# One core, two decode attention blocks: the V product as a loop of four passes, and projections over two banks

## The chip, the core and the metric

The kernel runs on one core of a Trainium2 chip. Five engines work beside each other and meet only at semaphores: TensorE (PE in the profile; its weight loads are listed apart as PEld), VectorE (DVE), ScalarE (ACT), GpSimd (POOL) and SyncE (SP). Here SyncE issues every transfer. The time of a run is what the device takes for one execution, in microseconds (us).

## What is computed

Two independent blocks, A and B, do the same with their own weights and caches. Each takes one new token for two batch entries, projects it to 32 query heads, attends over 8192 cached positions for each head and batch entry, and projects the result back; the two outputs stand side by side.

```python
q = (x @ wq).reshape(B, Sq, H, Dh).transpose(0, 2, 1, 3)     # B=2, Sq=1, D=640, H=32, Dh=192
scores = jnp.einsum("bhqd,bhkd->bhqk", q, k_cache) * (Dh ** -0.5)   # 8192 keys
p = softmax(scores, axis=-1)
o = jnp.einsum("bhqk,bhkd->bhqd", p, v_cache)
out = o.transpose(0, 2, 1, 3).reshape(B, Sq, H * Dh) @ wo
```

Every head has its own keys and values, and there is one query for each, so the caches are read once: 64 units of two heads and one batch entry, each with 6144 KB of K and 6144 KB of V, in bfloat16.

## The kernel before

**Units.** A unit u is two heads of one batch entry; u runs from 0 to 63, block A first. The 128 partitions hold 64 for each of the two heads; each partition holds 128 positions of 192 values.

**Buffers and loads.** Three buffers of 6144 KB each take the loads in the order k0, k1, v0, k2, v1, k3, v2 and so on. The list is written out, and load i waits until load i-3 has been used up (`done(i - NBUF)`): for K that is the unit's last product on VectorE (`dve_mul`, line 288), for V its product on TensorE (`pe_pv`, line 379). The first K load goes out at once. The loads k1 and v0 wait for the 16th and the 32nd projection instead, since their buffers hold the projection weights until then. The output weights `wo` come last, into buffers as these come free. All of them are issued by SyncE from line 247.

**Projections** (before the units). For each of 32 pairs of heads `pe_q` (line 357) makes five matmuls into one PSUM bank. VectorE copies two quarters of the bank to `qall` (`dve_qx`, line 278), and then ScalarE the other two (`act_q`, line 283). The banks are taken in turn from the list `qps`, which has four: the three score banks and `outps`. The projection hp waits for ScalarE's copy of hp-4, by the key `("qa", hp - NQ)` with `NQ = len(qps)`. On each engine this runs as a hardware loop, four pairs of heads in a turn, and the address of `wq` is taken from a register.

**One unit.** VectorE multiplies K by q in four chunks (line 288; two product buffers). TensorE sums each chunk with 12 matmuls against the identity (`pe_sum`, line 365), and VectorE reduces the result to scores (line 292). Then come the maximum (line 298), the maximum over partitions on GpSimd (line 269), and the exponential on ScalarE with sums over rows in `rs` (line 327). TensorE makes the denominator with `pe_l` (line 371), and the weighted sum of V with `pe_pv`: 64 matmuls, with 34 columns of `pb` as weights and 384 columns of V moving. VectorE and ScalarE put the result together (lines 303, 306, 309, 312).

**The order on TensorE** is fixed by a table of slots: in slot u the four chunk sums of unit u, then `pe_l` and `pe_pv` of unit u-1. Slots run in a hardware loop of three units a turn, since the buffers come round in threes; inside it all addresses of the chunk sums and of `pe_pv` are constants. A wait inside a loop is against a register, worked out from the turn's number (`_emit`, line 110; the loop itself is line 65).

**The end.** After the last K the products with V of units 62 and 63 remain, then `pe_turn` (line 393), which transposes the heads' results, and the output projections `pe_out` (line 407), block A and then block B. Between the two, `pe_idle` (line 415) makes eight matmuls whose result nobody reads.

Of the kernel before, what the change touches and what calls it, by code (L numbers as in the profile page):

```python
# [9 lines left out]
F32 = mybir.dt.float32  # L10


class _Stream:
# [93 lines left out]
    def _emit(self, eng, ops, it=None, steps=None):  # L107
        for fn, need, inc, _ in ops:
            for sid, (sem, val) in need.items():
                eng.wait_ge(sem, val if it is None else it * steps[sid] + val)  # L110
            if fn is None:
                continue
            ins = fn(eng)
            if inc:
                ins.then_inc(self.sem, inc)


def build_kernel(nc, blocks, out):
# [6 lines left out]
    NCH = T // TC  # L125
    TJ = T // 2
# [7 lines left out]
    NU = NP * B  # L134
    LASTU = NU - 1
    scale = float(Dh) ** -0.5
    NBUF = 3
    MP = 34
    JB = 16
    QW = 2 * Dh  # L140
# [6 lines left out]
    with ExitStack() as es:  # L147
        sb = lambda name, shape, dt: es.enter_context(nc.sbuf_tensor(name, shape, dt))
# [5 lines left out]
        ones = sb("ones", [128, 1], F32)  # L154
        big = sb("big", [128, NBUF * BUFE + 2 * PRODE], BF16)
        qall = sb("qall", [128, NU, Dh], BF16)
        pb = [sb(f"pb{i}", [128, 2 * T], BF16) for i in range(3)]
# [3 lines left out]
        mp = [sb(f"mp{i}", [128, 2], F32) for i in range(3)]  # L161
        mg = [sb(f"mg{i}", [128, 2], F32) for i in range(3)]
        nb = [sb(f"nb{i}", [128, 1], F32) for i in range(3)]
        rs = [sb(f"rs{i}", [128, 2], F32) for i in range(3)]
        ident = sb("ident", [128, 128], BF16)
        tri = sb("tri", [HP, HP + 1], BF16)
        place = sb("place", [2, 256], BF16)
# [4 lines left out]
        ops = [ps(f"ops{i}", [128, 512], F32) for i in range(3)]  # L172
        scps = [ps(f"scps{i}", [128, TC, DG], F32) for i in range(3)]
        outps = ps("outps", [128, 512], F32)
        oTps = ps("oTps", [128, 512], F32)
        qbank = [t[:].rearrange("p a b -> p (a b)") for t in scps]
        oacc = [outps[:], qbank[(LASTU * NCH + 1) % 3]]
        qps = qbank + [outps[:]]
        NQ = len(qps)

        kv = [big[:, i * BUFE:(i + 1) * BUFE].rearrange("p (t d) -> p t d", d=Dh) for i in range(NBUF)]
# [33 lines left out]
        buf = {}  # L215
# [8 lines left out]
        woA, wo0, wo1 = bk * BUFE, b62 * BUFE, b63 * BUFE  # L224
# [13 lines left out]
        def key(name, *idx):  # L238
            return (name,) + tuple(idx)

        def back(name, u, c, n):
            i = u * NCH + c - n
            return (name, i // NCH, i % NCH) if i >= 0 else None
# [24 lines left out]
        def pool_ar(u):  # L268
            return lambda eng: eng.partition_all_reduce(mg[u % 3][:], mp[u % 3][:], 128, bass.bass_isa.ReduceOp.max)  # L269
# [16 lines left out]
        def dve_mul(u, c):  # L286
            t = kv[buf["k", u]]
            return lambda eng: eng.tensor_tensor(prod[c % 2], t[:, c * TC:(c + 1) * TC, :],  # L288
                                                 qall[:, S_dve.at(u), :].broadcast_to([128, TC, Dh]), ALU.mult)

        def dve_red(u, c):
            return lambda eng: eng.tensor_reduce(sc[u % 3][:, c * TC:(c + 1) * TC], scps[(u * NCH + c) % 3][:], AXL.X, ALU.add)  # L292

        def dve_max(u):
            def fn(eng):
                for s in range(2):
                    r = slice(64 * s, 64 * s + 64)
                    ins = eng.tensor_reduce(mp[u % 3][r, s:s + 1], sc[u % 3][r, :], AXL.X, ALU.max)  # L298
                return ins
            return fn  # L300

        def dve_rc(u):
            return lambda eng: eng.reciprocal(rc[u % 3][:], ops[u % 3][0:2, QW:QW + 1])  # L303

        def dve_ohi(u):
            return lambda eng: eng.tensor_copy(o_hi[:], ops[u % 3][32:34, Dh:QW])  # L306
# [7 lines left out]
        def act_nb(u):  # L314
            def fn(eng):
                for s in range(2):
                    r = slice(64 * s, 64 * s + 64)
                    ins = eng.activation(nb[u % 3][r, :], mg[u % 3][r, s:s + 1], ACTF.Identity, scale=-scale)  # L318
                return ins
            return fn  # L320
# [41 lines left out]
        def pe_sum(u, c):  # L362
            def fn(eng):
                for j in range(NJ):
                    ins = eng.matmul(scps[(u * NCH + c) % 3][:], ident[:], prod[c % 2][:, :, j * DG:(j + 1) * DG],  # L365
                                     start=(j == 0), stop=(j == NJ - 1))
                return ins
            return fn

        def pe_l(u):  # L370
            return lambda eng: eng.matmul(ops[u % 3][0:2, QW:QW + 1], rs[u % 3][:], ones[:], start=True, stop=True)  # L371

        def pe_pv(u):
            vv = kv[buf["v", u]].rearrange("p (j a) d -> p j (a d)", a=2)

            def fn(eng):
                for j in range(TJ):
                    j0s = 4 * JB * (j // JB) + 2 * (j % JB)
                    ins = eng.matmul(ops[u % 3][0:MP, 0:QW], pb[u % 3][:, j0s:j0s + MP], vv[:, j, :],  # L379
                                     start=(j == 0), stop=(j == TJ - 1))  # L380
                return ins
            return fn

        def pe_turn(heads, blks):
# [15 lines left out]
        def pe_out(n):  # L400
# [8 lines left out]
                                         start=(i == 0), stop=(i == WR - 1))  # L409
                return ins  # L410
            return fn

        def pe_idle(eng):
            for i in range(8):
                ins = eng.matmul(ops[(LASTU + 1) % 3][:], ident[:], big[:, woA + 512 * i:woA + 512 * (i + 1)], start=True, stop=True)
            return ins

        NSLOT = NU + 8
        tabs = {e: {} for e in ("dve", "act", "pe", "pool")}
# [1 line left out]
        def put(eng, slot, order, fn, waits, sig, tag=None):  # L421
            t = tabs[eng].setdefault(slot, [])
            t.append((order, len(t), fn, waits, sig, tag))
# [14 lines left out]
        for u in range(NU):  # L438
            for c in range(NCH):
                w = [("k", u), ("pq", NP - 1), ("qa", NP - 1), ("qx", NP - 1), back("s", u, c, 2)]  # L440
                slot, order = (0, 9.2) if (u, c) == (1, 0) else (u, 2 + 2 * c)
                put("dve", slot, order, dve_mul(u, c), w, ("m", u, c), ("m", c, u % 3))
                put("dve", u, 5 + 2 * c if c < NCH - 1 else 9.5, dve_red(u, c),
                    [("s", u, c), key("mx", u - 3), key("exp", u - 3)], ("r", u, c), ("r", c, u % 3))
                put("pe", u, 0.1 * c, pe_sum(u, c),
                    [("m", u, c), ("os", -2) if (u, c) == (1, 0) else None, back("r", u, c, 3), ("id1",), ("qx", NP - 1), ("qa", NP - 1)], ("s", u, c), ("s", c, u % 3))
            put("dve", u, 12, dve_max(u), [("r", u, NCH - 1), key("ar", u - 3), ("init",)], ("mx", u), ("mx", u % 3))
            put("pool", u, 0, pool_ar(u), [("mx", u), key("nb", u - 3)], ("ar", u), ("ar", u % 3))
            put("act", u, 0, act_nb(u), [("ar", u), key("exp", u - 3)], ("nb", u), ("nb", u % 3))
            put("act", u, 1, act_exp(u), [("nb", u), key("pv", u - 3), key("l", u - 3), ("init",)], ("exp", u), ("exp", u % 3))  # L450
            w0 = [("exp", u), key("os", u - 3), key("rc", u - 3), ("init",)]
            pslot = u + 1
            pe_o = 2
            put("pe", pslot, pe_o, pe_l(u), w0, ("l", u), ("l", u % 3))
            put("pe", pslot, pe_o + 0.1, pe_pv(u), [("v", u)], ("pv", u), ("pv", u % 3, buf["v", u]))
            put("dve", u + 2, 20, dve_rc(u), [("pv", u), key("of", u - 3)], ("rc", u), ("rc", u % 3))
            put("dve", u + 2, 21, dve_ohi(u), [("pv", u), key("os", u - 1)], ("oh", u), ("oh", u % 3))
            put("dve", u + 2, 22, dve_osum(u), [("oh", u), key("of", u - 1)], ("os", u), ("os", u % 3))
            put("act", u + 2, 4, act_of(u), [("os", u), ("rc", u)], ("of", u), ("of", u % 3))

        put("pe", 0, -1, None, [("init",)], None)
        E2 = NU + 2
# [10 lines left out]
        for n, p in enumerate(pieces):  # L473
# [1 line left out]
            if p[0]:  # L475
                w.append(("r", LASTU, 1))
            put("pe", E2, 0.01 * n if n <= NA else 2 + 0.01 * n, pe_out(n), w, ("f", n))
        put("pe", E2, 1, pe_idle, [("of", LASTU)], None)
        for blk, n in enumerate((NA, len(pieces) - 1)):
            put("act", E2, 9 + blk, out_half(blk, 0), [("f", n)], ("oev", blk, 0))  # L480
            put("dve", E2 + 2, 30 + blk, out_half(blk, 1), [("f", n)], ("oev", blk, 1))
# [32 lines left out]
        for n in range(128 // HP):  # L514
# [9 lines left out]
            "dve": lambda u: [("m", u, 0), ("m", u, 1), ("r", u, 0), ("m", u, 2), ("r", u, 1), ("m", u, 3),  # L524
                              ("r", u, 2), ("r", u, 3), ("mx", u), ("rc", u - 2), ("oh", u - 2), ("os", u - 2)],
            "act": lambda u: [("nb", u), ("exp", u), ("of", u - 2)],
            "pe": lambda u: [("s", u, c) for c in range(NCH)] + [("l", u - 1), ("pv", u - 1)],
            "pool": lambda u: [("ar", u)],
        }
        pre, post = {}, {}  # L530
        for name, keys in per_unit.items():
            pre[keys(0)[0]] = [k for u in (-3, -2, -1) for k in keys(u)]
            for u in range(3):
                late = [k for k in keys(u) if k[1] < 0]
                if late:
                    post[[k for k in keys(u) if k[1] >= 0][-1]] = late

        for name, S in (("dve", S_dve), ("act", S_act), ("pe", S_pe), ("pool", S_pool)):
            for slot in sorted(tabs[name]):
                for _, _, fn, waits, sig, tag in sorted(tabs[name][slot], key=lambda e: (e[0], e[1])):  # L540
                    S.add(fn, waits=waits, sig=sig, tag=(slot, tag if tag is not None else object()),
                          pre=pre.get(sig, ()), post=post.get(sig, ()))
# [73 lines left out]
```

## Time and profile before

| what | value |
|---|---|
| time, median of 3 runs | 1936.92 us (1936.66 to 1936.93) |
| span of the profiled execution, first to last instruction | 1935.4 us |
| bytes moved, mean rate | 836.91 MB, 432 GB/s |
| share of the span that the DMA queue's packets took | 99.9% |
| TensorE matmuls busy | 1501.1 us (78%) |
| VectorE busy | 1122.5 us (58%) |
| mean granted TensorE clock | 0.956 |

The device time of the profiled execution is not listed apart from its span. The runs are 1.3 to 1.5 us longer than that span; this is what lies around the first and last instruction.

A row of a timeline gives start, length (both us), engine, line, operation, output and inputs, the number of instructions, and in brackets the idle time before it and what ended that. A row for a line of the kernel gives the shortest, median and longest duration in ns and where in the span the first and the last instruction started. Names ending in q (PEldq, SPq) are an engine's sequencer: register operations, branches and the issue of transfers, which do not count as busy.

### The profile page before, as it was taken

What the parts mean: (1) busy time and instruction counts of PE and PEld (TensorE: products, weight loads), DVE (VectorE), ACT (ScalarE), POOL (GpSimd) and SP (SyncE); (2) the same over time, 40 slices, a digit from 0 to 9 for tenths busy, and PEclk for the clock granted to TensorE, in tenths of its full rate; (3) what the DMA queues carried; (4) which work ended last, traced back from release to release, by engine and by line L of the source; (5) the groups of instructions that cost most, each with busy time, mean ns of one, the idle gap of its engine ahead of it and who ended that gap; (6) DMA issues with size and microseconds to landing.
All of it is one profiled execution on the core that took longest, in us unless ns stands there. A gap on an engine that the chain in (4) does not pass through costs nothing.

```text
span 1935.4 us, 19060 instructions
## 1 busy us (share of the span) xinstructions
PE 1501.1 (78%) x7728; PEld 730.0 (38%) x7729; DVE 1122.5 (58%) x907; ACT 142.4 (7%) x519; POOL 28.5 (1%) x113
## 2 busy tenths in 40 slices
PE   5788878878878878877877877877877877877878
PEld 2334433433433433433433333433333433433434
DVE  4765565565565565565565565565565565565560
ACT  3100000000000000000000000000000000000000
POOL 0000000000000000000000000000000000000000
PEclk9899999999999999999999999999999999999998
DMA  9999999999999999999999999999999999999999
GB/s 423 424 435 437 431 434 437 432 433 437 436 429 436 437 430 435 436 432 433 437 435 431 436 435 430 436 437 430 435 437 430 434 438 435 430 436 436 429 436 394
DMA packets 19754, 836.91 MB, mean 432 GB/s; under 512 B 2200, under 2 KB 2336, under 8 KB 2720
## 3 DMA queue, kind: packets, MB, share of 16 engines
q1 hardware_dynamic: 19744, 836.78, 99.9%
q8 instruction: 6, 0.10, 0.0%
q14 instruction: 4, 0.03, 0.0%
HBM read 836.77 MB, written 0.01 MB: 432 GB/s over the span
## 4 chain that ended last, share of the span: by engine, by line
DMA 49%; PE 28%; DVE 17%; issue 5%; DVEq 0%; SPq 0%; ACT 0%; ACTq 0%
DMA big<-in_B_k_cache_dram 25%; DMA big<-in_A_k_cache_dram 22%; PE ops L379 18%; DVE big L288 15%; PE scps L365 8%; DVE sc L292 2%; DMA big<-in_B_wo_dram 1%; PE scps L357 1%; DMA xw<-in_B_x_dram 1%; PE outps L357 0%; PE ops L371 0%; DVEq L288 0%; DVE qall L278 0%; SPq L247 0%; PE scps L407 0%
## 5 line engine op out<-in xcount | busy, mean ns | idle before, releaser
L288 DVE TENSOR_TENSOR big<-big,qall 128x6144 bf16<-128x6144 bf16 x256 | 852.8, 3351 | 526.6 <-DMA big<-in_B_k_cache_dram 278.7
L365 PE MATMUL scps<-big,ident 128*128 128x512 bf16 x3072 | 771.8, 408 | 401.1 <-DVE big L288 398.7
L379 PE MATMUL ops<-big,pb 128*34 128x384 bf16 x4096 | 676.8, 326 | 0.0
L365 PEld LDWEIGHTS scps<-big,ident 128*128 128x128 bf16 x3072 | 301.1, 104 | 865.1 <-DVE big L288 491.0
L379 PEld LDWEIGHTS ops<-big,pb 128*34 128x34 bf16 x4096 | 395.5, 98 | 258.7
L292 DVE TENSOR_REDUCE sc<-scps 128x32 f32<-128x512 f32 x256 | 175.8, 687 | 192.5 <-PE scps L365 192.5
L318 ACT ACTIVATE nb<-mg 64x1 f32<-64x1 f32 x128 | 25.8, 201 | 1706.8 <-POOL mg L269 1706.1
L327 ACT ACTIVATE pb<-sc,nb 64x128 bf16<-64x128 f32 x128 | 55.8, 436 | 7.8
L269 POOL PARTITION_ALL_REDUCE mg<-mp x64 | 25.7, 402 | 1857.9 <-DVE mp L298 1857.9
L298 DVE TENSOR_REDUCE mp<-sc 64x1 f32<-64x128 f32 x128 | 35.9, 280 | 8.3
L312 ACT ACTIVATE qall<-o_sum,rc 2x192 f32 (+1 forms) x64 | 29.0, 453 | 20.7 <-DVE o_sum L309 19.1
L309 DVE TENSOR_TENSOR o_sum<-ops,o_hi 2x192 f32<-2x192 f32 x64 | 22.1, 345 | 7.7
L357 PE MATMUL scps<-big,xw 128*128 x120 | 23.2, 351 | 2.2 <-DVE xw L274 2.2
L327 ACT ACTIVATION_READ_ACCUMULATOR pb<-sc,nb 64x1 f32 x128 | 23.7, 185 | 0.0
L306 DVE COPY o_hi<-ops 2x192 f32<-2x192 f32 x64 | 22.3, 349 | 2.0
L303 DVE RECIPROCAL rc<-ops 2x1 f32<-2x1 f32 x64 | 10.0, 156 | 21.3 <-PE ops L379 19.4
L278 DVE CAST qall<-scps 64x192 f32 x48 | 17.0, 355 | 6.5 <-PE scps L357 4.5
L283 ACT ACTIVATE qall<-scps 64x192 f32 x48 | 15.6, 324 | 30.1 <-DVE qall L278 27.8
L348 PE MATMUL oTps<-ident,xw 4*128 4x4 bf16 x5 | 0.4, 178 | 21.7 <-DMA xw<-in_B_x_dram 21.7
L357 PEld LDWEIGHTS scps<-big,xw 128*128 128x128 bf16 x120 | 12.4, 103 | 11.4 <-issue 5.2
L371 PEld LDWEIGHTS ops<-ones,rs 128*2 128x2 f32 x128 | 5.5, 82 | 26.9 <-issue 26.9
L407 PE MATMUL outps<-big,oT 128*2 128x320 bf16 x96 | 9.5, 375 | 5.6 <-DMA big<-in_A_wo_dram 5.6
(36 smaller groups left out, 67.6 us busy)
## 6 DMA issues: line engine op xcount, KB each, us to landing
big<-in_A_k_cache_dram SPq DMA_DIRECT2D x32, 6144.0 KB, 28.9
big<-in_A_v_cache_dram SPq DMA_DIRECT2D x32, 6144.0 KB, 27.9
big<-in_B_k_cache_dram SPq DMA_DIRECT2D x32, 6144.0 KB, 29.4
big<-in_B_v_cache_dram SPq DMA_DIRECT2D x32, 6144.0 KB, 28.2
big<-in_B_wq_dram SPq DMA_DIRECT2D x1, 7680.0 KB, 37.2
big<-in_A_wo_dram SPq DMA_DIRECT2D x1, 7680.0 KB, 30.1
big<-in_A_wq_dram SPq DMA_DIRECT2D x1, 7168.0 KB, 20.2
big<-in_B_wo_dram SPq DMA_DIRECT2D x1, 4640.0 KB, 30.4
```

The source lines that it names most:

```text
L269: return lambda eng: eng.partition_all_reduce(mg[u % 3][:], mp[u % 3][:], 128, bass.bass_isa.ReduceOp.max)
L288: return lambda eng: eng.tensor_tensor(prod[c % 2], t[:, c * TC:(c + 1) * TC, :], qall[:, S_dve.at(u), :].broadcast_to([128, TC, Dh]), ALU ...
L292: return lambda eng: eng.tensor_reduce(sc[u % 3][:, c * TC:(c + 1) * TC], scps[(u * NCH + c) % 3][:], AXL.X, ALU.add)
L298: ins = eng.tensor_reduce(mp[u % 3][r, s:s + 1], sc[u % 3][r, :], AXL.X, ALU.max)
L306: return lambda eng: eng.tensor_copy(o_hi[:], ops[u % 3][32:34, Dh:QW])
L309: return lambda eng: eng.tensor_tensor(o_sum[:], ops[u % 3][0:2, 0:Dh], o_hi[:], ALU.add)
L312: return lambda eng: eng.activation(qall[0:2, S_act.at(u), :], o_sum[:].unsqueeze(1), ACTF.Identity, scale=rc[u % 3][:])
L318: ins = eng.activation(nb[u % 3][r, :], mg[u % 3][r, s:s + 1], ACTF.Identity, scale=-scale)
L327: ins = eng.activation(dst, sc[u % 3][r, :].rearrange("p (g j a) -> p g a j", j=JB, a=2), ACTF.Exp, bias=nb[u % 3][r, :], scale=scale, acc ...
L357: ins = eng.matmul(qps[hp % NQ][:, 0:QW], xbc[:, blk, c, :], wq_t[blk][:, c, S_pe.at(off, QW, QW)], start=(c == 0), stop=(c == DC - 1))
L365: ins = eng.matmul(scps[(u * NCH + c) % 3][:], ident[:], prod[c % 2][:, :, j * DG:(j + 1) * DG], start=(j == 0), stop=(j == NJ - 1))
L379: ins = eng.matmul(ops[u % 3][0:MP, 0:QW], pb[u % 3][:, j0s:j0s + MP], vv[:, j, :], start=(j == 0), stop=(j == TJ - 1))
```

## The change

Two parts that touch each other only in the order of TensorE's work, and some small ones.

- `pe_pv` becomes a hardware loop of four passes over 16 matmuls, inside the loop over units. The addresses of `pb` (the weights) and of V (the moving operand) are worked out from the pass's register for every matmul. No matmul of it starts or ends an accumulation. Instead `pe_l`, which comes just ahead, opens the bank: it now writes 34 rows, so `rs` has 34 columns of which 32 stay zero. The loop's last matmul signals once in each pass, so a V product counts four signals instead of one.
- The wait for V moves from `pe_pv` to `pe_l`, the instruction ahead of it.
- `qps` has two banks instead of four; projection hp waits for ScalarE's copy of hp-2, and the projection loops have two pairs of heads in a turn.
- `pe_idle` is taken out.

```diff
@@ _Stream._emit @@
-                ins.then_inc(self.sem, inc)
+                ins.then_inc(self.sem, inc // getattr(fn, "turns", 1))
@@ build_kernel @@
-        rs = [sb(f"rs{i}", [128, 2], F32) for i in range(3)]
+        rs = [sb(f"rs{i}", [128, MP], F32) for i in range(3)]
...
-        qps = qbank + [outps[:]]
+        qps = qbank[:2]
         NQ = len(qps)
...
         def pe_l(u):
-            return lambda eng: eng.matmul(ops[u % 3][0:2, QW:QW + 1], rs[u % 3][:], ones[:], start=True, stop=True)
+            return lambda eng: eng.matmul(ops[u % 3][0:MP, QW:QW + 1], rs[u % 3][:], ones[:], start=True, stop=True)
 
         def pe_pv(u):
             vv = kv[buf["v", u]].rearrange("p (j a) d -> p j (a d)", a=2)
 
             def fn(eng):
-                for j in range(TJ):
-                    j0s = 4 * JB * (j // JB) + 2 * (j % JB)
-                    ins = eng.matmul(ops[u % 3][0:MP, 0:QW], pb[u % 3][:, j0s:j0s + MP], vv[:, j, :],
-                                     start=(j == 0), stop=(j == TJ - 1))
-                return ins
+                with eng.Fori(0, TJ // JB) as g:
+                    for j in range(JB):
+                        ins = eng.matmul(ops[u % 3][0:MP, 0:QW], pb[u % 3][:, bass.ds(g * (4 * JB) + 2 * j, MP)],
+                                         vv[:, bass.ds(g * JB + j, 1), :], start=False, stop=False, skip_group_check=True)
+                return ins
+
+            fn.turns = TJ // JB
             return fn
...
-        def pe_idle(eng):
-            for i in range(8):
-                ins = eng.matmul(ops[(LASTU + 1) % 3][:], ident[:], big[:, woA + 512 * i:woA + 512 * (i + 1)], start=True, stop=True)
-            return ins
...
-            put("pe", pslot, pe_o, pe_l(u), w0, ("l", u), ("l", u % 3))
-            put("pe", pslot, pe_o + 0.1, pe_pv(u), [("v", u)], ("pv", u), ("pv", u % 3, buf["v", u]))
+            put("pe", pslot, pe_o, pe_l(u), w0 + [("v", u)], ("l", u), ("l", u % 3))
+            put("pe", pslot, pe_o + 0.1, pe_pv(u), [], ("pv", u), ("pv", u % 3, buf["v", u]))
...
-        put("pe", E2, 1, pe_idle, [("of", LASTU)], None)
...
-            "pe": lambda u: [("s", u, c) for c in range(NCH)] + [("l", u - 1), ("pv", u - 1)],
+            "pe": lambda u: [("s", u, c) for c in range(NCH)] + [("l", u - 1)] + [("pv", u - 1, i) for i in range(1, TJ // JB)] + [("pv", u - 1)],
...
+        for u in range(NU):
+            pre[("pv", u)] = [("pv", u, i) for i in range(1, TJ // JB)]
```

## The prediction

> **What bounds the kernel now.** I read the page first: engines, DMA queue, span.
>
> ```profile
> span 1935.4 us, 19060 instructions
> PE 1501.1 (78%) x7728; PEld 730.0 (38%) x7729; DVE 1122.5 (58%) x907; ACT 142.4 (7%) x519; POOL 28.5 (1%) x113
> q1 hardware_dynamic: 19744, 836.78, 99.9%
> big<-in_A_wq_dram SPq DMA_DIRECT2D x1, 512.0 KB, 3.7
> ```
>
> Transfers fill the span, so TensorE's 78% is cover, as long as it stays under the period of the loads. Next I read the timeline from unit 2 on, VectorE's first product of a unit being the moment its K is there.
>
> ```profile
> 89.26 0.33 SPq L247 DMA_DIRECT2D big<-in_A_v_cache_dram  x1
> 89.29 2.76 PE L365 MATMUL scps<-big,ident 128*128 128x512 bf16 x12 [1.10 <-DVE big L288]
> ...
> 98.77 6.62 DVE L288 TENSOR_TENSOR big<-big,qall 128x6144 bf16<-128x6144 bf16 x2 [5.38 <-DMA big<-in_A_k_cache_dram]
> ```
>
> And the timeline of the last unit:
>
> ```profile
> 1867.81 6.63 DVE L288 TENSOR_TENSOR big<-big,qall 128x6144 bf16<-128x6144 bf16 x2 [7.98 <-DMA big<-in_B_k_cache_dram]
> 1871.22 2.76 PE L365 MATMUL scps<-big,ident 128*128 128x512 bf16 x12 [3.23 <-DVE big L288]
> 1874.35 0.68 DVE L292 TENSOR_REDUCE sc<-scps 128x32 f32<-128x512 f32 x1
> 1874.95 3.35 DVE L288 TENSOR_TENSOR big<-big,qall 128x6144 bf16<-128x6144 bf16 x1
> 1878.36 2.76 PE L365 MATMUL scps<-big,ident 128*128 128x512 bf16 x12 [1.10 <-DVE big L288]
> 1882.22 2.76 PE L365 MATMUL scps<-big,ident 128*128 128x512 bf16 x12 [1.10 <-DVE big L288]
> 1885.04 10.57 PE L379 MATMUL ops<-big,pb 128*34 128x384 bf16 x64
> 1895.54 1.51 PE L393 MATMUL oTps<-qall,place 2*32 2x96 bf16 x64
> ```
>
> From unit 2 (98.77) to unit 63 (1867.81) a unit takes (1867.81 - 98.77)/61 = 29.0 us, two loads of 14.5. Of these TensorE needs, from K's arrival, 3.4 until its first sum, 13.8 to the end of the sums, 10.6 for the V product: 27.8. It is 1.2 us from the next K, and 4.6 us (1.2 + 3.4) from its next sum. A V product longer by more than that is late.
>
> **The projections over two banks.** What is added is a wait: hp for ScalarE's copy of hp-2. Behind it on TensorE stand all later projections; for them wait both copying engines, the loads k1 (16th projection) and v0 (32nd), and the first product of unit 0. The timeline of this stage:
>
> ```profile
> 24.29 4.98 PE L357 MATMUL scps<-big,xw 128*128 x15 [2.18 <-DVE xw L274]
> ...
> 46.58 2.61 PE L357 MATMUL scps<-big,xw 128*128 x15
> 46.84 0.72 DVE L278 CAST qall<-outps 64x192 f32 x2
> 47.69 0.66 ACT L283 ACTIVATE qall<-outps 64x192 f32 x2 [0.15 <-DVE qall L278]
> 47.74 2.33 DVE L278 CAST qall<-scps 64x192 f32 x6 [0.18 <-PE scps L357]
> 48.60 2.27 ACT L283 ACTIVATE qall<-scps 64x192 f32 x6 [0.24 <-DVE qall L278]
> ...
> 49.89 2.61 PE L357 MATMUL scps<-big,xw 128*128 x15
> ...
> 52.34 0.98 PE L357 MATMUL outps<-big,xw 128*128 x5
> ...
> 55.19 6.63 DVE L288 TENSOR_TENSOR big<-big,qall 128x6144 bf16<-128x6144 bf16 x2 [0.99 <-ACT qall L283]
> ```
>
> Now four pairs of heads take 49.89 - 46.58 = 3.31 us, 0.83 each, TensorE's own pace. With two banks the way round one bank sets it: matmuls until VectorE's copy 47.74 - 46.58 = 1.16, copies until ScalarE 48.60 - 47.74 = 0.86, ScalarE's two copies 0.66, and the handover to a TensorE held by a register instruction, 0.15 as from VectorE to ScalarE (between 0.05 and 0.3): 2.83 us for two. The first matmuls run at half pace (4.98 us for 15 against 2.61), which makes the first two rounds 0.8 longer. The 31st projection starts at 24.29 + 2 x 3.63 + 13 x 2.83 = 68.3, the 32nd 0.8 later at 69.1, and the first product as long behind it as now (55.19 - 52.34 = 2.85): 72.0 instead of 55.2, **16.8 us late**. TensorE is busy 57% of a round; if that left it at half clock, all rounds would take 3.63, another 10 us. Against it speaks a stretch with 63%:
>
> ```profile
> 69.00:72.00 3.00, 1.90 (x10) 0.70 (x8) 3.00 (x2) 0.00 (x0) 0.00 (x0) 1.00 1.21 524
> ```
>
> k1 (47.5 instead of 40.2) is still early. For v0, k2 and v1 the queued loads are the cover. The 512 KB load of wq landed 3.7 us after issue, 1.2 of them at the pace of the K loads; so a load into an empty queue needs 2.5 + 14.5 = 17.0. v1 is due 14.5 after k2 (98.8), at 113.3, and so has to go out by 96.3; now it goes out at 89.3, 7.0 early. Of the 16.8 therefore 9.8 us become an idle DMA queue, if nothing else is late.
>
> **The V product as a loop.** What is added is sequencer work: for each matmul two addresses, for each pass an addition and a branch. Rows for the sequencer: the projections' address instruction (all of them, then five in a row), the end of a turn of the loop over units, and the two additions ahead of the last V products.
>
> ```profile
> L357 PEldq FUSED_REGOPS  x160: 46/46/60, 24.2 to 52.5; - x160
> ...
> L357 PEldq FUSED_REGOPS  x5: 46/46/46, 47.2 to 47.7; - x5
> ...
> L65 PEldq ALU_OP  x1: 32/32/32, 1806.9 to 1806.9; - x1
> L65 PEldq COMPARE_BRANCH  x1: 207/207/207, 1807.0 to 1807.0; - x1
> L65 PEldq FUSED_REGOPS  x1: 50/50/50, 1807.3 to 1807.3; - x1
> ...
> L110 PEldq ALU_OP  x2: 32/32/32, 1882.3 to 1882.4; - x2
> ```
>
> A projection matmul has one register address, one such instruction, and takes the sequencer (47.7 - 47.2)/4 = 0.125 us; under the 0.165 that a matmul of 384 columns streams (10.57/64), so today it is hidden. The second address: at least one more instruction's own 0.046, so 0.17 in all; at most a second full pair with the longest instruction twice, 2 x (0.125 + 0.014) = 0.28. I take nearly a whole second one: V's address has a multiplication by the row and a buffer offset more than the projections', so 0.06 to 0.07, and some 0.06 to 0.07 around it, as between the two additions (0.1 from start to start, 0.032 long): **0.255 us a matmul**, and 0.36 a pass (0.03 + 0.21 and about 0.06 after each). One V product then takes the sequencer T = 64 x 0.255 + 4 x 0.36 = 17.8 us.
>
> [...]
>
> Part of T lies under the sums: the two additions run at 1882.3 and 1882.4, right after the last sum has started at 1882.22, so the sequencer gains 2.7 us on it. A period of TensorE from first sum to first sum, when it is itself the late one: sum 2.8, reduction 0.6 and product 3.4 until the third sum (6.8), then 3.9 (1882.22 - 1878.36) to the fourth: 10.7; 0.4 until the loop's first matmul; T; 0.3 to the next sum. P = 10.7 + 0.4 + 17.8 + 0.3 = **29.2 us against the loads' 29.0**: the cover is just used up, TensorE becomes the bound, and the slip of the projections is not caught up. The point of decision is 0.252 us a matmul; each 0.01 above costs 0.64 a unit, 40 us in all.
>
> **Edits without a price.** The 34 columns of `rs` lengthen three fills ahead of all work of TensorE, which waits for x anyway, and one weight load a unit by a part of the 0.125 that a whole matmul costs. The wait for V moves one instruction forward; the same instructions stand behind it. Nobody waits for the three extra signals. [...]
>
> **The sum.** First K-sums end as late as the projections: the fourth sum of unit 1 starts at 89.3 + 16.8 = 106.1. To that of unit 63: 62 x 29.16 = 1808, so 1914. V product 62: + 18.6; transposing 1.5; V product 63, 1.5 of it ahead: 16.9; results and transpose 1.9; output of A and of B, 7.0 each as B's now:
>
> ```profile
> L407 PE MATMUL scps<-big,oT x96: 297/299/299, 1926.4 to 1933.3; 128*2 128x320 bf16 x96
> ```
>
> and 1.7 to store: 1968.6 against a span of 1935.4. The runs are 1.5 longer than the span: **1970 us**, 33 us or 1.7% slower.
>
> **Rivals.**
> - *The loop stays hidden* (below 0.252 us a matmul; both addresses in one instruction would do). Then only the idle DMA at the start is left: 1936.9 + 9.8 = 1947, or up to 4.6 more, TensorE's slack in a unit, when the longer loop holds back k3 on the way: 1951. For it: P is over the loads' period by 0.2 us only. Against: one address alone takes 0.125. 0.26.
> - *Both parts dear*: 0.276 a matmul, T = 19.1, P = 30.5: 62 x 1.34 + 2 x 1.3 = 86 over the forecast, 2056. For it: no row shows weights with a register address. 0.12.
> - *Not slower.* The loads queued ahead absorb the projections, and the loop is hidden. That holds if the slip is under 7.0, so a round under (62.2 - 2.85 - 0.8 - 24.3)/15 = 2.28 us. Matmuls 0.81 and copies 0.72 and 0.66 alone are 2.19, and each handover now shown takes 0.15 to 0.35. Time 1937. 0.06.
> - *Faster*, by something that the trace does not show: 0.02.
>
> **How the numbers follow.** My forecast 0.54, the rivals as given. What a measurement here can tell from no change is 0.2%, 3.9 us. Slower: 0.54 + 0.26 + 0.12 = 0.92; same 0.06; faster 0.02. The range runs from the first rival's lower end, 1945, to 0.271 us a matmul, 2035; it leaves out the dear end and the case without a loss.
>
> **What would show it.** In the timeline after: v0 issued near 70 (53 now, at the end of the 32nd projection), the first product near 72; projections with ScalarE as releaser. In the rows: some 128 to 190 register instructions a unit at line 379, LDWEIGHTS there with gaps put down to issue. V products of 15 to 16 us instead of 10.6; VectorE no longer waiting for K but for the product buffers, and a period over 29.0. Wrong would be: V products still of 10.6 us (first rival), or a DMA queue still 99.9% busy.

## The result and the profile after

The changed kernel takes 1952.89 us (median of 4 runs, 1952.55 to 1953.26) against 1936.85 us before (the three runs listed ahead and a fourth): a ratio of 1.0083, 95% interval 1.0069 to 1.0097. It is 16 us slower. The range on record holds that; the likeliest case, 1970 us with TensorE as the bound, does not describe it. The page of the changed kernel, with the rows that answer to those read before (in the row "GB/s" 40 equal slices of the span):

```profile
span 1951.8 us, 27861 instructions
PE 1694.5 (87%) x7721; PEld 697.2 (36%) x7721; DVE 1124.2 (58%) x907; ACT 142.4 (7%) x519; POOL 31.8 (2%) x113
GB/s 419 369 372 426 429 434 435 435 435 434 433 435 430 432 435 434 433 433 435 435 435 435 433 434 432 432 432 435 435 431 435 435 435 435 435 432 435 430 434 382
q1 hardware_dynamic: 19744, 836.78, 99.3%
PE 64%; DVE 21%; issue 9%; DMA 6%; ACT 0%; DVEq 0%; ACTq 0%; SPq 0%
```

There are 8800 instructions more, nearly all of them the address work and the branches of the loop. The last row is the chain of what ended last; in the kernel before it was:

```profile
DMA 49%; PE 28%; DVE 17%; issue 5%; DVEq 0%; SPq 0%; ACT 0%; ACTq 0%
```

It now runs through TensorE for 64% and through DMA for 6%. Read alone, that says that TensorE has become the bound. The rates say something else: only the second, third and a little of the fourth slice are low, and from then on the loads run at 429 to 435 GB/s, as before, up to the last slice. A chain of waits shows who was last at each step; it does not show that the period has become longer.

The projections and the first product in the timeline:

```profile
64.54 1.99 PE L357 MATMUL scps<-big,xw 128*128 x10 [0.81 <-ACT qall L283]
...
67.37 1.96 PE L357 MATMUL scps<-big,xw 128*128 x10 [0.84 <-ACT qall L283]
...
69.36 0.33 SPq L247 DMA_DIRECT2D big<-in_A_v_cache_dram  x1
...
71.21 6.63 DVE L288 TENSOR_TENSOR big<-big,qall 128x6144 bf16<-128x6144 bf16 x2 [0.99 <-ACT qall L283]
```

A round of two projections takes 67.37 - 64.54 = 2.83 us, and ScalarE is the releaser. The load of v0 goes out at 69.36, the first product starts at 71.21, which is 16.0 us later than before. Then the V product of unit 0, the load k3 that waits for it, and units 3 and 4, followed by the last unit:

```profile
107.77 6.56 PE L379 MATMUL ops<-big,pb 128*34 x32
...
114.63 4.19 PE L379 MATMUL ops<-big,pb 128*34 x16 [0.30 <-issue]
119.11 4.18 PE L379 MATMUL ops<-big,pb 128*34 x16 [0.30 <-issue]
...
123.33 0.33 SPq L247 DMA_DIRECT2D big<-in_A_k_cache_dram  x1
...
141.83 6.63 DVE L288 TENSOR_TENSOR big<-big,qall 128x6144 bf16<-128x6144 bf16 x2 [2.79 <-DMA big<-in_A_k_cache_dram]
...
152.53 5.35 PE L365 MATMUL scps<-big,ident 128*128 128x512 bf16 x24
...
172.72 6.63 DVE L288 TENSOR_TENSOR big<-big,qall 128x6144 bf16<-128x6144 bf16 x2 [4.46 <-DMA big<-in_A_k_cache_dram]
...
1883.71 6.63 DVE L288 TENSOR_TENSOR big<-big,qall 128x6144 bf16<-128x6144 bf16 x2 [9.32 <-DMA big<-in_B_k_cache_dram]
...
1887.43 2.76 PE L365 MATMUL scps<-big,ident 128*128 128x512 bf16 x12
```

And units 3 and 4 in the timeline of the kernel before:

```profile
127.96 6.63 DVE L288 TENSOR_TENSOR big<-big,qall 128x6144 bf16<-128x6144 bf16 x2 [9.62 <-DMA big<-in_A_k_cache_dram]
...
156.89 6.63 DVE L288 TENSOR_TENSOR big<-big,qall 128x6144 bf16<-128x6144 bf16 x2 [7.68 <-DMA big<-in_A_k_cache_dram]
```

The V product takes 123.29 - 107.77 = 15.5 us instead of 10.6, with gaps of 0.30 put down to issue between the passes. K of unit 3 is 141.83 - 127.96 = 13.9 us late, K of unit 4 172.72 - 156.89 = 15.8 and K of unit 63 1883.71 - 1867.81 = 15.9 us. So the loss is there by unit 4, and it does not grow over the next 59 units: (1883.71 - 172.72)/59 = 29.00 us a unit, the pace of the loads, as before. TensorE gains on them: from a unit's first product to its first sum there are 10.7 us in unit 3 (152.53 - 141.83) and 3.7 in unit 63, where 3.4 is the least, the product itself. So TensorE is late in every unit, which is what the chain shows, but a little less late each time; at the last unit the two are 0.3 us apart.

### The profile page after: what moved, and what is told of

Same layout as the page of the kernel before. It is cut to its first block, busy times and chain, and to the rows that moved or that the text cites. A ratio compares the mean times of both kernels' runs of the same rounds, so it can differ in the third digit from the quotient of the medians.

```text
span 1951.8 us, 27861 instructions
## 1 busy us (share of the span) xinstructions
PE 1694.5 (87%) x7721; PEld 697.2 (36%) x7721; DVE 1124.2 (58%) x907; ACT 142.4 (7%) x519; POOL 31.8 (2%) x113
## 4 chain that ended last, share of the span: by engine, by line
PE 64%; DVE 21%; issue 9%; DMA 6%; ACT 0%; DVEq 0%; ACTq 0%; SPq 0%
PE ops L379 45%; DVE big L288 18%; PE scps L365 17%; DMA big<-in_B_k_cache_dram 3%; DVE sc L292 2%; DMA big<-in_A_k_cache_dram 2%; DMA xw<-in_B_x_dram 1%; PE scps L357 1%; PE ops L371 0%; DVE qall L278 0%; ACT qall L283 0%; PE outps L409 0%; PE scps L409 0%; PE oTps L395 0%; DVEq L278 0%
## 5 line engine op out<-in xcount | busy, mean ns | idle before, releaser
L379 PE MATMUL ops<-big,pb 128*34 x4096 | 943.9, 329 | 38.0 <-issue 38.0
L365 PE MATMUL scps<-big,ident 128*128 128x512 bf16 x3072 | 700.9, 381 | 180.0 <-DVE big L288 169.7
L379 PEld LDWEIGHTS ops<-big,pb 128*34 x4096 | 382.2, 94 | 585.6 <-issue 508.3
L365 PEld LDWEIGHTS scps<-big,ident 128*128 128x128 bf16 x3072 | 285.3, 98 | 580.4 <-DVE big L288 233.3
L357 PE MATMUL scps<-big,xw 128*128 x160 | 33.1, 341 | 14.5 <-ACT qall L283 12.0
L278 DVE CAST qall<-scps 64x192 f32 x64 | 22.7, 355 | 24.1 <-PE scps L357 23.6
L357 PEld LDWEIGHTS scps<-big,xw 128*128 128x128 bf16 x160 | 15.9, 99 | 31.5 <-issue 27.4
L283 ACT ACTIVATE qall<-scps 64x192 f32 x64 | 20.8, 325 | 47.7 <-DVE qall L278 47.4
L371 PEld LDWEIGHTS ops<-ones,rs 128*34 128x34 f32 x128 | 9.0, 109 | 26.9 <-issue 26.9
L371 PE MATMUL ops<-ones,rs 128*34 128x1 f32 x128 | 14.5, 182 | 0.0
```

The source lines that it names most:

```text
L278: return lambda eng: eng.tensor_copy(qall[ro, S_dve.at(B * hp + 1 - s, 1, B), :], qps[hp % NQ][ri, s * Dh:(s + 1) * Dh].unsqueeze(1))
L357: ins = eng.matmul(qps[hp % NQ][:, 0:QW], xbc[:, blk, c, :], wq_t[blk][:, c, S_pe.at(off, QW, QW)], start=(c == 0), stop=(c == DC - 1))
L371: return lambda eng: eng.matmul(ops[u % 3][0:MP, QW:QW + 1], rs[u % 3][:], ones[:], start=True, stop=True)
L379: ins = eng.matmul(ops[u % 3][0:MP, 0:QW], pb[u % 3][:, bass.ds(g * (4 * JB) + 2 * j, MP)], vv[:, bass.ds(g * JB + j, 1), :], start=False, ...
```

## Experiments

All times are beside runs of the kernel before on the same chip, whose median was 1936.85 to 1936.94 us. "K of unit 63 late" is the start of that unit's first product against 1867.81 before: what an idle DMA queue has cost up to there. What the time has beyond it was lost at the end. The last two columns come from one execution of each kernel, the profiled one. For one address (1945.70 us, 8.8 over before) and for the change with the straight end (1952.44, 15.5 over) that was the fastest of four, so these two rows show no loss at the end.

| kernel | time, us | ratio, 95% interval | over before | first product | K of unit 63 late |
|---|---|---|---|---|---|
| the change | 1952.89 | 1.0069 to 1.0097 | 16.0 | 71.2 | 15.9 |
| two banks alone | 1948.09 | 1.0038 to 1.0072 | 11.2 | 71.6 | 10.8 |
| one bank alone | 2015.93 | 1.0391 to 1.0426 | 79.0 | 140.8 | 79.0 |
| loop, four banks | 1941.77 | 1.0015 to 1.0035 | 4.8 | 55.1 | 0.1 |
| loop, four banks, straight end | 1937.13 | 0.9992 to 1.0011 | 0.2 | 55.2 | 0.4 |
| the change, straight end | 1953.91 | 1.0073 to 1.0107 | 17.0 | 71.2 | 15.9 |
| loop, three banks | 1943.86 | 1.0023 to 1.0048 | 6.9 | 57.9 | 2.6 |
| one address | 1947.58 | 1.0039 to 1.0073 | 10.7 | 71.7 | 8.7 |
| two passes | 1951.88 | 1.0059 to 1.0092 | 15.0 | 72.2 | 15.4 |
| a turn added | 1973.62 | 1.0172 to 1.0206 | 36.7 | 71.4 | 27.7 |
| five turns, four banks | 2053.68 | 1.0583 to 1.0619 | 116.8 | 55.2 | 103.1 |
| small edits alone | 1936.97 | 0.9991 to 1.0011 | 0.0 | 55.2 | 0 |

### The projections alone

Two banks, all else as before:

```diff
-        qps = qbank + [outps[:]]
+        qps = qbank[:2]
```

> The kernel before with two projection banks and nothing else. Theory (the loads lose their cover at the start): the first product at 71.2 as in the changed kernel, 16.0 us late; V products stay 10.6 us; the DMA queue loses about 10 us once, between v0 and v1, and the time is 1947 (1945 to 1949). Rival (the whole of the loss belongs to the projections): 1953. Rival (queued loads absorb them): 1937.

```profile
71.62 6.63 DVE L288 TENSOR_TENSOR big<-big,qall 128x6144 bf16<-128x6144 bf16 x2 [1.00 <-ACT qall L283]
...
108.53 10.57 PE L379 MATMUL ops<-big,pb 128*34 128x384 bf16 x64
...
119.14 0.33 SPq L247 DMA_DIRECT2D big<-in_A_k_cache_dram  x1
...
138.40 6.63 DVE L288 TENSOR_TENSOR big<-big,qall 128x6144 bf16<-128x6144 bf16 x2 [3.62 <-DMA big<-in_A_k_cache_dram]
...
1878.57 6.63 DVE L288 TENSOR_TENSOR big<-big,qall 128x6144 bf16<-128x6144 bf16 x2 [7.10 <-DMA big<-in_B_k_cache_dram]
```

Measured 1948.09, as expected. The first product slips by 16.4 us, K of unit 3 comes 138.40 - 127.96 = 10.4 us late, and K of unit 63 10.8. The loads queued ahead cover 16.4 - 10.8 = 5.6 us of the slip, and the rest stays to the end. The V product is the old one, and k3 goes out as soon as it ends, 4.2 us earlier than with the loop (119.14 against 123.33).

One bank, to make the slip much larger:

```diff
-        qps = qbank + [outps[:]]
+        qps = qbank[:1]
```

> The kernel before, with one bank for the projections and the V product as it was. The way round the bank then holds every projection: matmuls 1.16 until VectorE's copy, 0.86 until ScalarE's, 0.66 for its copies, 0.15 for the handover, so a round of 2.83 us for one projection instead of two, 31 rounds from 24.29: first product at about 24.3 + 0.8 + 31 x 2.83 + 0.8 + 2.85 = 116.5 (55.2 before, 71.6 with two banks). Theory (the loads queued ahead cover the first 5 to 6 us of a slip, every further one is an idle DMA queue, to the end): slip 61.3 less 5.6, 1937 + 55.7 = 1992.5 (1989 to 1996). Rival (part of a slip is caught up over the 64 units, because TensorE and VectorE have slack in each of them): under 1985.

```profile
129.82 1.78 PE L357 MATMUL scps<-big,xw 128*128 x5 [1.84 <-ACT qall L283]
...
133.45 1.78 PE L357 MATMUL scps<-big,xw 128*128 x5 [1.84 <-ACT qall L283]
...
140.75 6.63 DVE L288 TENSOR_TENSOR big<-big,qall 128x6144 bf16<-128x6144 bf16 x2 [0.99 <-ACT qall L283]
```

The number was missed by 23 us, and the theory held. The miss is in the round: 133.45 - 129.82 = 3.63 us, not 2.83, since the five matmuls take 1.78 us instead of 0.98 and do so up to the last projection. 31 rounds of 0.8 more are 24.8 us; one 0.8 of them was in the expectation, and the slip is 85.5 - 61.3 = 24.2 us more than expected. Of the slip, now 85.5 us (140.75 - 55.19), 6.5 are covered, and the time is 79.0 longer: K of unit 63 is 79.0 us late, and nothing was caught up over 64 units, although TensorE and VectorE have slack in each of them.

### The loop alone, and where its cost lies

The changed kernel with the four banks of before:

```diff
-        qps = qbank[:2]
+        qps = qbank + [outps[:]]
```

> The changed kernel with the four projection banks of before. Theory (the loop's period of 28.9 us fits just under the 29.0 of two loads): V products 15 us, the time 1937 (1936 to 1939). Rival (TensorE is the bound, as I forecast, or the loop alone costs time): 1942 to 1960.

The expectation of no loss was missed: 4.8 us. The timeline of its end:

```profile
1867.88 6.63 DVE L288 TENSOR_TENSOR big<-big,qall 128x6144 bf16<-128x6144 bf16 x2 [5.26 <-DMA big<-in_B_k_cache_dram]
...
1875.64 5.35 PE L365 MATMUL scps<-big,ident 128*128 128x512 bf16 x24
...
1905.95 8.63 PE L379 MATMUL ops<-big,pb 128*34 x32
...
1919.48 4.17 PE L379 MATMUL ops<-big,pb 128*34 x16 [0.33 <-issue]
...
1925.41 6.68 PE L409 MATMUL outps<-big,oT 128*2 128x320 bf16 x96
...
1931.93 6.69 PE L409 MATMUL scps<-big,oT 128*2 128x320 bf16 x96
```

And the outputs in the timeline of the kernel before:

```profile
1915.13 9.46 PE L407 MATMUL outps<-big,oT 128*2 128x320 bf16 x96 [5.62 <-DMA big<-in_A_wo_dram]
...
1932.15 1.44 PE L407 MATMUL scps<-big,oT 128*2 128x320 bf16 x16 [0.19 <-DMA big<-in_B_wo_dram]
```

K of unit 63 is on time (1867.88 against 1867.81), so nothing was lost over 64 units. But TensorE begins its sums 7.8 us behind it instead of 3.4, and after the last load its own work counts in full: two long V products, the last from 1905.95 to 1923.65 in 17.7 us, with no sums ahead of it that could hide a part of its address work, then both outputs without a pause to 1938.62. Before, TensorE waited 5.6 us there for the output weights and ended at 1933.59. The cover was the last loads, and it is 5 us too short.

To show it, the V products of the last four units were written as 64 matmuls with constant addresses again, and the loop over units ends three units earlier; once with four banks, once in the changed kernel:

```diff
+            def straight(eng):
+                for j in range(TJ):
+                    j0s = 4 * JB * (j // JB) + 2 * (j % JB)
+                    ins = eng.matmul(ops[u % 3][0:MP, 0:QW], pb[u % 3][:, j0s:j0s + MP], vv[:, j, :],
+                                     start=False, stop=False, skip_group_check=True)
+                return ins
+            if u >= NU - 4:
+                return straight
...
-            put("pe", pslot, pe_o + 0.1, pe_pv(u), [], ("pv", u), ("pv", u % 3, buf["v", u]))
+            put("pe", pslot, pe_o + 0.1, pe_pv(u), [], ("pv", u), ("pv", u % 3, buf["v", u], u >= NU - 4))
```

> The loop of passes with four banks for the projections, but the V products of the last four units (60 to 63) as 64 matmuls with constant addresses, so that the loop over units ends at slot 60. Theory (with four banks the loop costs nothing while loads run, and its 4.8 us are paid in the tail alone: TensorE 8.2 us behind the last K instead of 3.9, and two long V products in series): the time of the kernel before, 1937 (1936.5 to 1937.8). Rival (the loss builds up along the 64 units): it stays at 1941 to 1942.

> The changed kernel (two banks, loop of passes), but the V products of the last four units as 64 matmuls with constant addresses. Theory (15.2 of its 16 us are a DMA queue that is late from the first units on, and only about 1 us is paid in the tail): 1952 (1951.6 to 1952.5). Rival (the parts add up: 11.2 for the projections everywhere and 4.8 for the loop in the tail): 1948.

The end of the first of the two in the timeline:

```profile
1899.54 10.56 PE L386 MATMUL ops<-big,pb 128*34 128x384 bf16 x64
...
1915.12 9.55 PE L418 MATMUL outps<-big,oT 128*2 128x320 bf16 x96 [3.20 <-DMA big<-in_A_wo_dram]
```

With four banks the time is that of the kernel before, 1937.13 us (0.9992 to 1.0011): sixty units with the loop cost nothing, and the outputs wait for their weights again, until 1915.12 (1915.13 before). In the changed kernel the same edit brings nothing that can be measured: 1953.91, with runs from 1952.44 to 1955.27. That is 1.4 us above the range expected, for which no trace gives a cause, but 1948, the rival, is ruled out. So the parts' losses, 11.2 and 4.8, add up to 16.0 only by chance: in the changed kernel the loop costs its 5 us at the start, where it holds k3 back, and the end has nearly its cover again, since the output weights come 16 us later too. The profiled span is 0.8 us shorter with the straight end (1951.0 against 1951.8), but each is of one run only.

Three banks (`qps = qbank[:3]`) in the changed kernel:

> The changed kernel with three projection banks. A round of three takes 2.83 us, 0.94 for a pair of heads against 0.83 with four: first product about 3 to 4 us late. Theory (a slip under the cover of 5 to 7 us costs nothing by itself, and the longer V product takes some more of the cover): 1937 to 1940. Rival (every us of the slip is lost): 1941 or more.

Missed as well: 6.9 us. For 2.6 of them, a late K, the rival was right: the first product slips by 2.7, and with the longer V product next to nothing of it is covered. The rest is the end, as with four banks.

### What of the loop costs

One address instead of two: the weights' address is a constant, so three quarters of the V products are made with the first pass's probabilities; only the address of V comes from the register.

```diff
-                        ins = eng.matmul(ops[u % 3][0:MP, 0:QW], pb[u % 3][:, bass.ds(g * (4 * JB) + 2 * j, MP)],
+                        ins = eng.matmul(ops[u % 3][0:MP, 0:QW], pb[u % 3][:, 2 * j:2 * j + MP],
```

> The changed kernel, but the loop takes the weights of the first pass in all four passes, a constant address, so the product of the other three quarters of V is made with wrong weights; V's address still comes from the register. Price of the second address: with one register address a matmul should take the sequencer 0.13 to 0.15 us, under the 0.165 that it streams, so V products go back to 10.6 to 11.5 us. Theory (the start loses 10 us for the projections and the rest because V products 0 to 5 are late): 1947 to 1948, as with two banks alone. Rival (the rest is not the V product's length): 1953.

Two passes of 32 matmuls instead of four of 16:

> The changed kernel with two passes over 32 matmuls instead of four over 16. Each pass that is saved takes 0.5 us off the sequencer, so V products 14.2 us and TensorE's period 27.9. Theory (a shorter V product gives back part of the late start): 1950 to 1952, under the 1952.9 of four passes. Rival (its length plays no part while it fits): 1952.9.

The V products in the groups of the changed kernel (busy time and mean ns of one; idle time before them and what ended it); then one V product of the kernel with one address, in its timeline; then the group of that with two passes:

```profile
L379 PE MATMUL ops<-big,pb 128*34 x4096 | 943.9, 329 | 38.0 <-issue 38.0
```

```profile
1228.92 10.56 PE L379 MATMUL ops<-big,pb 128*34 x64
```

```profile
L379 PE MATMUL ops<-big,pb 128*34 x4096 | 915.0, 329 | 19.0 <-issue 19.0
```

With one address a V product takes 10.6 us, as with constants: passes, branches and one address are hidden, and the time is that of two banks alone. It is the second address that makes the sequencer slower than the array: with both, a pass of sixteen matmuls takes it 4.5 us, and sixteen matmuls stream for 16 x 0.165 = 2.6. The register instructions of line 379 count the same way, first with two addresses, then with one:

```profile
L379 PEldq FUSED_REGOPS  x6676: 42/74/89, 105.5 to 1934.6; - x197
```

```profile
L379 PEldq FUSED_REGOPS  x3840: 55/64/84, 104.2 to 1917.2; - x192
```

With 1260 additions of 32 ns that the first has besides, these are (6676 + 1260)/256 = 31 in a pass of sixteen matmuls against 3840/256 = 15. No kernel takes the weights' address alone from a register; that it would cost no more than that of V is argued from these counts and not measured.

Half the passes halve the idle time put down to issue (19.0 against 38.0 us over 64 units). A V product takes 14.7 us (1175.45 to 1190.14; 14.2 expected), where the changed kernel has 15.5. By estimate from that, and from the changed kernel's period of 28.94 us, TensorE's own period is 28.2 (27.9 expected), so it catches up with the loads: in unit 38 its first sum starts 3.4 us behind the first product (1161.66 - 1158.25), the least there is, and the chain goes back to DMA:

```profile
DMA 38%; PE 35%; DVE 18%; issue 8%; ACT 0%; DVEq 0%; ACTq 0%; SPq 0%
```

Yet the time, 1951.88, differs from the changed kernel's by less than the intervals, so between the theory and the rival here nothing is settled. What it shows is that the 64% of the chain on TensorE were not what set the changed kernel's time: a period shorter by 0.7 us would then have been worth some 62 x 0.7 = 43 us.

### The point of decision

If the loads set the period while TensorE needs a little less, a little more sequencer work must tip it. An empty loop of one turn ahead of each V product:

```diff
+                with eng.Fori(0, 1):
+                    pass
                 with eng.Fori(0, TJ // JB) as g:
```

> The changed kernel with an empty loop of one turn ahead of each V product: one move, one addition and one branch not taken more for the sequencer, 0.3 us. Theory (TensorE's period is 28.9 and the loads' 29.0, so there is 0.1 us of cover left): period 29.2, TensorE becomes the bound, 62 x 0.24 = 15 us longer than the changed kernel: 1965 to 1972. Rival (cover of 1 us or more is left): 1953 to 1954.

And of five turns, with four banks:

> Four banks, the loop of four passes, and an empty loop of five turns ahead of each V product: 1.6 to 1.8 us more for the sequencer. Theory (past the edge each us counts once a unit): period 30.6, 1937 + 62 x 1.6 = 2036 (2025 to 2050). Rival (the sequencer runs ahead far enough to hide it): 1937 to 1945.

Two units of each in the timeline, the first kernel with one turn:

```profile
1224.32 6.63 DVE L288 TENSOR_TENSOR big<-big,qall 128x6144 bf16<-128x6144 bf16 x2 [3.59 <-DMA big<-in_B_k_cache_dram]
...
1895.50 6.63 DVE L288 TENSOR_TENSOR big<-big,qall 128x6144 bf16<-128x6144 bf16 x2 [2.84 <-DMA big<-in_B_k_cache_dram]
```

```profile
1201.95 6.63 DVE L288 TENSOR_TENSOR big<-big,qall 128x6144 bf16<-128x6144 bf16 x2 [1.03 <-DMA big<-in_B_k_cache_dram]
...
1970.94 6.62 DVE L288 TENSOR_TENSOR big<-big,qall 128x6144 bf16<-128x6144 bf16 x2 [1.65 <-DMA big<-in_B_k_cache_dram]
```

Both were slower than their ranges, by 1.6 and 3.7 us, and both rivals are out. With one turn the period is (1895.50 - 1224.32)/23 = 29.18 us, with five (1970.94 - 1201.95)/25 = 30.76, and no longer the loads' 29.0. The lateness now grows with every unit: K of unit 63 comes 27.7 and 103.1 us late, and what the times have beyond that, 9 and 14 us, is the end. VectorE still names DMA in its waits, but the loads are late because TensorE frees the buffers late: with five turns a K load of block B that goes out at 1861.20 is in use at 1878.43, 17.2 us later, with hardly a queue ahead of it; before, these loads land 29.4 us after their issue (median). With one turn the time, 1973.62 us, is near the 1970 that the prediction gave for a period of 29.2: the mechanism exists, but the changed kernel is a quarter of a microsecond a unit short of it.

### The small edits

`rs` with 34 columns, the wait for V at `pe_l`, and no `pe_idle`, with the old V product and four banks:

> The kernel before with the small edits alone: 34 columns of row sums and 34 rows of the denominator's matmul, the wait for V one instruction earlier, no idle matmuls before block B's output. All theories: 1937, no change (within 1 us); a rival in which block B's output falls to half clock: 1939 to 1941.

1936.97 us (0.9991 to 1.0011): no price, as expected. Without `pe_idle` ahead of it, and after a wait of 2.65 us for its weights, block B's output took 299 ns a matmul, as before, so the half clock of the rival did not come. The 2 to 4 us of that rival were the author's estimate, and no run shows them for block B. Block A's output shows what a wait did: 9.46 us for its 96 matmuls before, behind a wait of 5.62 us, against 6.68 in the kernel with the loop and four banks, where it did not wait.

## Why the prediction was right or wrong

**What bounds the kernel, right.** The loads at 29.0 us a unit set the end before and after: K of unit 63 is 15.9 us late, of 16.0 us in the time.

**The projections, right.** Round 2.83 us forecast and measured; first product 72.0 forecast, 71.2 measured: the slower first rounds were priced 0.6 us high, and the projections began 0.4 earlier than before (23.89 against 24.29). The cover by the queued loads was forecast as 7.0 us; in the three kernels with a V product of the old length it was 5.6 (two banks), 6.5 (one bank) and 7.8 (one address: 16.5 of slip, 8.7 late). So the idle DMA of two banks came out as 10.8 and 8.7 us, around the 9.8 forecast. The scatter goes with the pace of the first sums, which the forecast took as fixed: from the first product of unit 0 to the fourth sum of unit 1 there are 34.1, 33.2 and 32.0 us in these three profiled executions. The half pace that the prediction weighed and left out, with rounds of 3.63, did not come with two banks; with one it did.

**The sequencer's work, right.** From the first sum of unit 43 to that of unit 44 in the changed kernel: first the rows of the passes' register instructions (line 377), then the timeline.

```profile
L377 PEldq FUSED_REGOPS  x4: 78/78/78, 1319.9 to 1333.4; - x4
...
L377 PEldq COMPARE_BRANCH  x4: 76/208/208, 1324.1 to 1337.6; - x4
L377 PEldq MOVE  x1: 29/29/29, 1319.8 to 1319.8; - x1
```

```profile
1308.87 5.35 PE L365 MATMUL scps<-big,ident 128*128 128x512 bf16 x24 [0.40 <-issue]
...
1319.55 2.76 PE L365 MATMUL scps<-big,ident 128*128 128x512 bf16 x12 [1.10 <-DVE big L288]
...
1337.81 0.39 PE L365 MATMUL scps<-big,ident 128*128 128x512 bf16 x1
```

A pass takes the sequencer (1333.4 - 1319.9)/3 = 4.5 us, forecast 16 x 0.255 + 0.36 = 4.44; from the first instruction (1319.8) to the end of the last branch (1337.6 + 0.1) it is T = 17.8 to 17.9 us, forecast 17.8. A branch that is taken has 207 to 208 ns, as in the row of 207 ns that the prediction went by, and the last one, not taken, 76. That the sum came out this close is in part luck: the prediction's own bounds for a matmul were 0.17 and 0.28 us, and it chose between them by an estimate.

**The comparison with the loads, wrong: the step that failed.** P = 10.7 + 0.4 + T + 0.3 = 29.2 put TensorE over 29.0. Measured, with the same parts: fourth sum after the first 1319.55 - 1308.87 = 10.68, then 0.3 to the loop's first instruction, T, and 0.1 to 0.2 to the next sum at 1337.81; together 1337.81 - 1308.87 = 28.94. Mis-sized were the two handovers, 0.4 and 0.3 in the prediction and some 0.4 together in the trace. With 28.94 TensorE is under the loads by not quite 0.1 us, and each unit gives some of its lateness back: that is why the slip of the projections does not grow, and why the likeliest case fell. Over all units, from the fourth sum of unit 1 to that of unit 63:

```profile
104.99 2.76 PE L365 MATMUL scps<-big,ident 128*128 128x512 bf16 x12 [1.10 <-DVE big L288]
...
1898.13 2.76 PE L365 MATMUL scps<-big,ident 128*128 128x512 bf16 x12 [1.10 <-DVE big L288]
```

The mean is (1898.13 - 104.99)/62 = 28.92, so 62 x (29.16 - 28.92) = 14.9 of the 16.8 us by which the sum was above the measured span (1968.6 against 1951.8) come from this step. Of its signs, a period over 29.0 and a VectorE that waits for the product buffers in place of K did not come. A margin of 0.2 us in 29 was finer than the handovers were known, so the rival on its other side deserved as much of the chance.

**The first rival, right in kind, short in size.** Not below 0.252 us a matmul, as it was put, but at 0.255, and not with V products of 10.6 us, its sign, but with 15.5, it is what happened: idle DMA at the start, and up to 4.6 us more where the longer V product holds back k3. It gave 1951 at most. Its terms as measured, with two banks alone for the first: idle DMA 10.8 instead of 9.8; k3 and what follows it 15.9 - 10.8 = 5.1 instead of 4.6; and 0.5 at the end (span 16.4 longer, of which 15.9 are the late K).

**The end, not priced where the loop is hidden.** The rival took V products hidden under loads as free up to the last instruction, but the last two have no load over them. In this change the late output weights cover it again; with four banks it is the whole loss, and both expectations that left it out, for four and three banks, were missed by 4 to 5 us.

**Settled or not.** Shown by runs: the projections' part, the second address as the cost of the loop (not which of the two is the dearer), the edge at 29.0, and the end as the place of the loop's loss with four banks. Open: in the kernel with four banks TensorE catches up more slowly than in the changed one (the 7.8 us of unit 63 were 8.1 in unit 44), from a period that is longer by less than 0.1 us. No kernel tried is faster than the one before.

## What to carry to other kernels

Where loads fill the span, as here with 29.0 us a unit, price a change by whether a load goes out later than its queue runs dry. Of the projections' slip 5.6 to 7.8 us were covered, and the rest, 8.7 to 79.0 us, was still there in full at unit 63. The longer engine was free as long as its own period stayed under that of the loads: sixty units with the loop of passes cost nothing (1937.13 us with four banks and the straight end), while with a turn added, at 29.18 us, every unit lost some more. When that comparison comes out within one per cent, the handovers at the edges decide it (0.7 us in the prediction, some 0.4 in the trace, for a margin of 0.2), so give both sides their chance, or measure the edge with a kernel that has a little more of the same work. Price the end by itself: with four banks the loop, hidden under the loads up to there, cost its 4.8 us behind the last one.

## What the runs showed that was not expected

- The number of addresses from registers decided. With one in each matmul (that of V) the V product kept 10.6 us; with two it took 15.5, and a pass of sixteen took the sequencer 4.5 us. With the weights at a constant address the loop cost nothing that could be measured (1947.58 us against 1948.09 with two banks alone).
- TensorE stayed at half pace for a whole stage. With one bank, five matmuls took 1.78 us of every 3.63 and never became faster, for 114 us; with two banks ten took 1.96 of 2.83, at full pace after the first rounds. The granted clock in the profile's row shows nothing of it; columns: window and length in us, TensorE's matmuls and weight loads in us and number, granted clock, DMA share, GB/s:

```profile
24.50:138.00 113.50, 56.08 (x158) 20.99 (x159) 1.00 0.38 163
```

  With one bank the half-pace bursts filled 49% of each round, with gaps of 1.84 us. In the changed kernel the first ten matmuls filled 3.38 of the first 3.63 us and full pace followed, which 1.96 us in every 2.83 (69%), with gaps of 0.84, then kept. What decides between the two paces, no run here shows. In the first sums of the changed kernel, from 74 to 78 us, the same column has 0.50 (fifteen of these matmuls took 5.60 us, where twelve take 2.76 later on), so it is not blind everywhere; ahead of the first sums the pace is to be read from the matmuls' own durations.
- TensorE's sequencer ran ahead of the array: the loop's first instruction stood 0.3 us behind the start of the last sum, and 17.8 us of address work showed as a V product of 15.5.
